# One token tile in the first block, global queries after it, and values' two parts in one matmul

## The chip, the cores and the metric

The kernel runs on one core of a Trainium2 chip. The metric is the device time of one execution in microseconds, from the first to the last instruction of that core with what lies around them; the median of several executions counts. The core's engines run side by side, each in its own order: TensorE (PE, with its weight loads as PEld), VectorE (DVE), ScalarE (ACT), GpSimd (POOL) and SyncE (SP), whose queue begins transfers. They wait for one another by semaphores.

## The reference

Windowed attention with global tokens is followed by a two-layer feed-forward over all 4352 tokens:

```python
k_all, v_all = concat([k_g, k_l]), concat([v_g, v_l])          # 8 batches, 8 heads, 32 global + 512 local, 64 wide
out_g = softmax(q_g @ k_all.T * scale) @ v_all                 # global queries see everything
s_ll  = where(|i - j| <= 32, q_l @ k_l.T * scale, -1e9)        # local queries see a window
out_l = softmax(concat([q_l @ k_g.T * scale, s_ll])) @ concat([v_g, v_l])
x = concat([out_g, out_l]) as (4352, 512)
h = x @ w_in                                                   # 512 -> 2048, weights drawn as float64
y = (h * sigmoid(h)) @ w_out                                   # 2048 -> 512
```

## The kernel before

The tokens are 34 tiles of the feed-forward (32 of 128 local tokens, two that gather the 128 global tokens of four batches each). The feed-forward takes them in blocks (`SIZES`): block 0 has two tiles, then ten of three, the last of two. A block runs 16 iterations f over the hidden width: `first_layer` makes h for 128 hidden units from four chunks, `second_layer` of the iteration before adds to one bank for each tile. Block 0 works in plain float32, whose matmuls the trace shows as two records each. Later blocks work on float32 split into a high and a low part (`w_hi`, `w_lo`, `xh`, `xl`), with three products per chunk in a faster format.

Attention is 128 steps k, a step being two heads (u = 0, 1) of one pair of the eight, for one tile of 128 queries; four steps make a tile and 16 a batch. A step loads `raw` (queries and keys) and `vraw`, makes scores s (`st_scores`, L345), a softmax with two exponentials (L353), turns the probabilities on TensorE (`st_turn`, t, L378 or L380) into `pt`, and multiplies with the values (`st_out`, o, L423). The 32 columns beside each 128 belong to the global queries' own share of that chunk, and are summed into `acc`. Steps before KF = 24 are whole: one float32 product. From 24 on values and probabilities are split, three products each (`vhi`, `vlo` against `pt_hi`, and `vhi` against `pt_lo`), 12 matmuls a step. Scores are split from 24 on too, in an earlier form up to ND = 28. Split steps carry `probs` through a transfer (`rr`), whole ones don't. For each batch the global queries' scores (`g_scores`, gs), softmax (`g_soft`) and turning (`g_turn`, gt and gu, into `pgt`) stand ahead of that batch's local steps; batches before GF = 2 are whole.

Weights come as float64 words, 32 halves of 512 KB. `load_weights` loads a half on SP's queue, ScalarE takes its upper words (L179), VectorE puts the bits together (L181, L182). `split_weights` then makes `w_hi` on ScalarE (L192) and `w_lo` on GpSimd (L193), after each iteration of block 0.

What sets the order: each piece of attention gets a due time, the pieces are sorted, and `fill` sets them between the feed-forward's matmuls, so that a block's iterations carry the steps of the next block. TensorE's order is that of the program; the other engines' instructions are ordered by a scheduler, except those that are held in program order. Ahead of block 0's matmuls stand the steps of its own tiles. PSUM banks for attention are one each for scores, turned tiles and values (with more of them before block 0 starts).

Of the kernel before, what the change touches and what calls it, by code (L numbers as in the profile page):

```python
# [20 lines left out]
P = 128  # L21
# [3 lines left out]
W = 224  # L25
# [27 lines left out]
MOVE0, TURN0 = (0.1, 0.8), (1.5, 3.6)  # L53
START = dict(head=0.55, gap=0.0, late=-0.65, first=1.8)
# [4 lines left out]
def attention_moe_kernel(ctx: ExitStack, tc: tile.TileContext, qk0_in, qk_in, v_in, gqk, wts, out):  # L59
# [102 lines left out]
    w_32, w_hi, w_lo, w_next = [], [], [], [0, 0]  # L162

    def load_weights():
        f, c0 = w_next
        if c0 == 0:
            w_32.append(const.tile([P, 2 * DM], F32, tag=f"ws{f + 1}", name=f"w{f}") if f + 1 < NF else xtiles(0)[1])
        w_next[:] = (f, DM) if c0 == 0 else (f + 1, 0)
        w = w_32[f][:, c0 : c0 + DM]
        raw = scratch(SCRATCH + (2 * f + c0 // DM) % (NF - SCRATCH), I32, f"raw_w{f}_{c0}")  # L170
        load = nc.sync.dma_start(out=raw, in_=wts[f, :, c0 : c0 + DM].bitcast(I32))
        if 2 * f + c0 // DM < NF - SCRATCH:
            tc.keep_in_program_order(load)

        words = raw.rearrange("p (n w) -> p n w", w=2)
        nc.scalar.activation(w, words[:, :, 1].bitcast(F32), AF.Prelu, scale=2.0**-112, alpha=-(2.0**32))  # L179
        wi, low = w.bitcast(U32), words[:, :, 0].bitcast(U32)  # L180
        nc.vector.tensor_scalar(out=low, in0=low, scalar1=29, scalar2=None, op0=ALU.logical_shift_right)  # L181
        nc.vector.scalar_tensor_tensor(out=wi, in0=wi, scalar=3, in1=low, op0=ALU.logical_shift_left,  # L182
                                       op1=ALU.bitwise_or)

    def split_weights(f):
        taken.add(f)
        w_hi.append(const.tile([P, 2 * DM], F32R, tag=f"wh{f}", name=f"w_hi{f}"))
        w_lo.append(const.tile([P, 2 * DM], F32R, tag=f"ws{f}", name=f"w_lo{f}"))
        for c0 in range(0, 2 * DM, DM):
            sl = slice(c0, c0 + DM)  # L190
            hi, lo, w = w_hi[f][:, sl], w_lo[f][:, sl], w_32[f][:, sl]
            nc.scalar.copy(out=hi, in_=w)  # L192
            nc.gpsimd.tensor_tensor(out=lo, in0=w, in1=hi.bitcast(F32), op=ALU.subtract)  # L193
# [20 lines left out]
    def g_scores(b, p):  # L214
        did(("scores", b, p), *([("turn" if b <= GF else "move", b - 1, p // 2)] if b else []))
# [36 lines left out]
    def g_move(b, hh):  # L252
# [4 lines left out]
        r1 = two.tile([P, SG], F32R, tag="rg", name=f"rg1_{b}_{hh}")  # L257
        nc.sync.dma_start(out=r0.bitcast(F32), in_=pgs[hh][:, : 4 * P])
        nc.sync.dma_start(out=r1.bitcast(F32), in_=pgs[hh][:, 4 * P :])
        state["rg", hh] = r0, r1  # L260

    def g_turn(b, hh):
        whole = b < GF
        if whole:
            r0, r1, idt = pgs[hh], pgs[hh][:, 4 * P :], ident.bitcast(F32)
        else:
            (r0, r1), idt = state.pop(("rg", hh)), ident
        did(("turn", b, hh), ("turn", b, 0) if hh else ("last", b - 1))
# [8 lines left out]
        nc.scalar.copy(out=pgt[:, 0:4, hs, :], in_=tb.rearrange("p (t h q) -> p t h q", t=4, h=4))  # L277
        tb = attbank("s", f"gu{b}_{hh}")
        nc.tensor.transpose(tb[:SG, :P] if whole else tb[:SG, :P].bitcast(F32R), r1, idt)
        nc.scalar.copy(out=pgt[:SG, 4, hs, :], in_=tb[:SG, :P].rearrange("p (h q) -> p h q", h=4))  # L280
# [4 lines left out]
    def st_load(k, b, c, pr):  # L285
        raw = raw_tile(f"raw{k}", k < KF)
# [6 lines left out]
    def st_vload(k, b, c, pr):  # L293
        if k < KF and k % 2:
            vraw = two.tile([P, 2, 2, D], F32, tag="vhi" if k % 4 == 1 else "vlo", name=f"vraw{k}")
# [5 lines left out]
    def st_split(k, b, c, pr):  # L301
        if k < KF:
            return
# [3 lines left out]
        if k < ND:  # L307
            n = QW + W
            nc.scalar.copy(out=qk[:, :n], in_=raw[:, :n])
            (nc.gpsimd if k < ND else nc.vector).tensor_tensor(out=klo[:, :n], in0=raw[:, :n], in1=qk[:, :n].bitcast(F32), op=ALU.subtract)  # L310
            return
        nc.scalar.copy(out=qk, in_=raw)  # L312
        (nc.gpsimd if k < ND else nc.vector).tensor_tensor(out=klo[:, :KW], in0=raw[:, QW:], in1=qk[:, QW:].bitcast(F32), op=ALU.subtract)
        nc.vector.tensor_tensor(out=qk[D:, :QW], in0=raw[D:, :QW], in1=qk[D:, :QW].bitcast(F32), op=ALU.subtract)

    def st_vsplit(k, b, c, pr):
# [3 lines left out]
        vhi = two.tile([P, 2, 2, D], F32R, tag="vhi", name=f"vhi{k}")  # L320
        vlo = two.tile([P, 2, 2, D], F32R, tag="vlo", name=f"vlo{k}")
# [3 lines left out]
        tiles["v", k] = vhi, vlo  # L325

    def st_scores(k, b, c, pr):
        if k < KF:
# [4 lines left out]
        for u in range(2):  # L333
            o = s[:, u * W : (u + 1) * W]
            qs = slice(u * P, (u + 1) * P)
            if k < KF:
                terms = [(raw[:, qs], raw[:, QW : QW + W])]
            elif k < ND:
                ks = slice(QW, QW + W)
                terms = [(qk[:, qs], qk[:, ks]), (qk[:, qs], klo[:, ks]), (klo[:, qs], qk[:, ks])]  # L340
# [27 lines left out]
    def st_turn(k, b, c, pr):  # L368
# [12 lines left out]
        t4 = t.rearrange("p (u a q) -> p u a q", u=2, a=2)  # L381
        if whole:
            pt = tiles["pt", k] = pt_whole(k)
            if c == NC - 1:
                nc.gpsimd.memset(pt[:, :, 1, P:], 0.0)
            nc.scalar.copy(out=pt[:, :, :, :P], in_=t4)
        else:
            pt_hi, pt_lo = pt_tiles(k)
            nc.scalar.copy(out=pt_hi[:, :, :, :P], in_=t4)
# [299 lines left out]
```

## Time and profile before

| | us |
|---|---|
| median of 3 runs (1088.55 to 1090.19) | 1089.91 |
| the profiled run | 1086.34 |
| its span, first to last instruction | 1084.6 |
| TensorE busy | 1053.5 (97%) |
| VectorE / ScalarE / GpSimd busy | 727.4 / 693.0 / 146.5 |

Matmuls overlap in the trace: the duration of one is not its price, and the price is read from the start of the next. A busy TensorE does not mean one at its peak. The chain of work that ended last is 93% TensorE over the span. Profiles show one execution; the sum in the prediction is made against its span.

### The profile page before, as it was taken

The page shows a single profiled execution, that of the slowest core. Times are in us where ns is not written, and L with a number is a line of the kernel's source. Part 1 is how long each engine was busy: PE and PEld are TensorE (multiplying, and loading weights), DVE is VectorE, ACT ScalarE, POOL GpSimd, SP SyncE. Part 2 cuts the span into 40 slices and gives each one's busy share as a digit, 9 for nine tenths or more (in the row PEclk, how much of TensorE's full clock was granted, in tenths as well). Part 3 has the DMA queues.
Part 4 walks back from the last instruction along what each step waited for, and adds up shares of the span by engine and source line. Part 5 has one row for each costly group of instructions (what it writes and reads, how often), then busy time and mean ns, then how long its engine had stood idle before and what let it go on. Part 6 is the DMA issues. An engine that isn't in the chain of part 4 may idle for free.

```text
span 1084.6 us, 20466 instructions
## 1 busy us (share of the span) xinstructions
PE 1053.5 (97%) x6568; PEld 934.9 (86%) x6568; DVE 727.4 (67%) x2367; ACT 693.0 (64%) x1845; POOL 146.5 (14%) x360
## 2 busy tenths in 40 slices
PE   6878999999999999999999999999999999999998
PEld 4645778989999999999999999998999999999997
DVE  5974355777677777666777877786778867753322
ACT  7875456767677766656766766776677776653232
POOL 3123542111100110000110100001000111000000
PEclk8989999999999999999999999999999999999999
DMA  9961112343334333332433433443344433310000
GB/s 351 380 189 59 57 59 76 119 146 125 111 112 142 124 107 115 116 115 82 140 110 122 149 111 109 138 135 108 111 141 125 141 114 112 112 60 20 1 30 20
DMA packets 69611, 127.29 MB, mean 117 GB/s; under 512 B 9344, under 2 KB 29312, under 8 KB 69504
## 3 DMA queue, kind: packets, MB, share of 16 engines
q1 hardware_dynamic: 69504, 125.99, 36.1%
q8 instruction: 52, 0.85, 0.3%
q14 instruction: 55, 0.45, 0.1%
HBM read 86.44 MB, written 8.91 MB: 88 GB/s over the span
## 4 chain that ended last, share of the span: by engine, by line
PE 93%; ACT 3%; DVE 2%; issue 1%; DMA 1%; ACTq 0%; DVEq 0%
PE h L563 33%; PE out L588 12%; PE out L590 11%; PE out L589 11%; PE o L423 10%; PE s L345 6%; PE t L380 3%; PE h L557 2%; PE out L586 2%; PE t L378 1%; DMA raw_w<-in_wts_dram 1%; PE gs L226 1%; PE gs L228 1%; ACT w_hi L192 1%; ACT w L179 1%
## 5 line engine op out<-in xcount | busy, mean ns | idle before, releaser
L563 PE MATMUL h<-xh,w_hi 128*128 128x384 f32 (+1 forms) x704 | 236.8, 336 | 0.0
L563 PE MATMUL h<-xh,w_lo 128*128 128x384 f32 (+1 forms) x704 | 233.5, 332 | 0.0
L563 PE MATMUL h<-xl,w_hi 128*128 128x384 f32 (+1 forms) x704 | 233.1, 331 | 0.0
L569 ACT ACTIVATE t<-h 128x384 f32<-128x384 f32 (+1 forms) x192 | 90.7, 472 | 207.3 <-PE h L563 189.4
L588 PE MATMUL out<-w_hi,gh 128*128 128x512 f32 x512 | 210.6, 411 | 0.0
L590 PE MATMUL out<-w_hi,gl 128*128 128x512 f32 x512 | 201.3, 393 | 0.0
L589 PE MATMUL out<-w_lo,gh 128*128 128x512 f32 x512 | 200.3, 391 | 0.0
L571 DVE SCALAR_TENSOR_TENSOR t<-t,h 128x384 f32<-128x384 f32 (+1 forms) x176 | 95.2, 541 | 132.6 <-ACT t L569 131.9
L563 PEld LDWEIGHTS h<-xl,w_hi 128*128 128x128 f32 x704 | 132.6, 188 | 5.4 <-issue 0.5
L563 PEld LDWEIGHTS h<-xh,w_hi 128*128 128x128 f32 x704 | 132.5, 188 | 5.4 <-issue 0.7
L400 POOL CAST pt_hi<-pgt 128x64 fp32r<-128x64 f32 (+1 forms) x132 | 39.1, 308 | 724.4 <-PE o L423 706.1
L563 PEld LDWEIGHTS h<-xh,w_lo 128*128 128x128 f32 x704 | 132.3, 188 | 0.0
L576 DVE TENSOR_TENSOR gl<-t,gh 128x384 fp32r<-128x384 f32 (+1 forms) x176 | 96.8, 550 | 46.6 <-PE out L590 42.5
L349 DVE CUSTOM_DVE_ANT_0 probs<-s,mask 128x224 f32<-128x224 f32 x244 | 85.0, 384 | 62.0 <-PE s L345 61.4
L353 ACT ACTIVATE probs<-probs,st 128x224 f32<-128x224 f32 x244 | 115.7, 475 | 11.2 <-DVE st L349 10.5
L590 PEld LDWEIGHTS out<-w_hi,gl 128*128 128x128 f32 x512 | 96.1, 188 | 22.3 <-DVE gl L576 0.3
L589 PEld LDWEIGHTS out<-w_lo,gh 128*128 128x128 f32 x512 | 97.0, 189 | 10.5
L588 PEld LDWEIGHTS out<-w_hi,gh 128*128 128x128 f32 x512 | 96.4, 188 | 10.6 <-ACT gh L575 0.4
L575 ACT CAST gh<-t 128x384 fp32r<-128x384 f32 (+1 forms) x176 | 88.3, 501 | 21.8 <-DVE t L571 17.3
L434 ACT CAST xh<-o 64x128 fp32r<-64x128 f32 x240 | 61.3, 256 | 42.5 <-PE o L423 29.4
L312 ACT CAST qk<-raw 128x704 fp32r<-128x704 f32 x100 | 78.2, 782 | 15.9 <-PE s L345 15.6
L435 DVE TENSOR_TENSOR xl<-o,xh 64x128 fp32r<-64x128 f32 x240 | 67.3, 280 | 30.9 <-ACT xh L434 27.4
(117 smaller groups left out, 1937.3 us busy)
## 6 DMA issues: line engine op xcount, KB each, us to landing
raw<-in_qk_dram SPq DMA_DIRECT2D x100, 352.0 KB, 3.0
rr<-probs SPq DMA_DIRECT2D x104, 256.0 KB, 2.3
raw_w<-in_wts_dram SPq DMA_DIRECT2D x32, 512.0 KB, 6.3
vraw<-in_v_dram SPq DMA_DIRECT2D x128, 128.0 KB, 2.4
raw_g<-in_gqk_dram SPq DMA_DIRECT2D x32, 304.0 KB, 2.9
out_dram<-o SPq DMA_DIRECT2D x32, 256.0 KB, 2.3
raw<-in_qk_dram SPq DMA_DIRECT2D x28, 240.0 KB, 4.8
rg<-pg SPq DMA_DIRECT2D x12, 256.0 KB, 2.4
```

Source lines behind the costliest of these rows:

```text
L312: nc.scalar.copy(out=qk, in_=raw)
L349: nc.vector.tensor_tensor_reduce(out=p[:, u, :W], in0=s[:, u * W : (u + 1) * W], in1=mask_of[c], scale=-SCALE, scalar=3.0e38, op0=ALU.add, ...
L353: nc.scalar.activation(p[:, u, :W], p[:, u, :W], AF.Exp, bias=st[:, u : u + 1], scale=-1.0, accum_out=st[:, 2 + u : 3 + u])
L423: nc.tensor.matmul(o[:D, u * wide : u * wide + m], v[:, a, u, :], pt[:, u, a, :m], start=(i == 0), stop=(i == len(terms) - 1))
L563: nc.tensor.matmul(h[:, :nt], wt, x[:, c, :nt], start=(i == 0), stop=(i == 3 * NCC - 1))
L569: nc.scalar.activation(t[:, :nt], h[:, :nt], AF.Tanh, scale=0.5)
L571: nc.vector.scalar_tensor_tensor(out=out[:, :nt], in0=t[:, :nt], scalar=1.0, in1=h[:, :nt], op0=ALU.add, op1=ALU.mult)
L575: nc.scalar.copy(out=gh[:, :nt], in_=t[:, :nt])
L576: nc.vector.tensor_tensor(out=gl[:, :nt], in0=t[:, :nt], in1=gh[:, :nt].bitcast(F32), op=ALU.subtract)
L588: nc.tensor.matmul(o, gh[:, sl], wh, start=(f == 0), stop=False)
L589: nc.tensor.matmul(o, gh[:, sl], wl, start=False, stop=False)
L590: nc.tensor.matmul(o, gl[:, sl], wh, start=False, stop=(f == NF - 1))
```

## The change

Block 0 takes one tile and the others three each. In `KF` 24 becomes 16 (steps 16 to 23 are split for values and probabilities), in `GF` 2 becomes 3, and scores stay whole up to step 27. The global queries of batch 0 come after block 0's own four steps, which leave their 32 columns out; `g_late` adds that share with eight small products. The values' high and low parts lie side by side in one tile `vv`, which one matmul takes as 128 stationary columns; the output's upper 64 rows hold the low part's product, and are added to the lower 64 through a tile `xs`. The last 32 keys of the global queries' probabilities are kept split in `pgh`, `pgl`, and no longer moved by a transfer of their own. Weight loads are begun by ScalarE on its own queue (`fetch_weights`) and joined later (`join_weights`), all held in program order; the weights' split begins at iteration 11 and goes on into block 1, one f an iteration.

```diff
-SIZES = (2, 3, 3, 3, 3, 3, 3, 3, 3, 3, 3, 2)
+SIZES = (1,) + (3,) * 11
-KF = 24
-GF = 2
+KF = 16
+GF = 3
-LOOK = 5
-FIRSTW, PACE, WAT = 2, 1.0, -1.5
+FETCH, LOOK = 4, 2
+SPLIT0, SPLITS = 11, 1.0
...
-        load = nc.sync.dma_start(out=raw, in_=wts[f, :, c0 : c0 + DM].bitcast(I32))
+        load = nc.scalar.dma_start(out=w_raw[i], in_=wts[i // 2, :, sl].bitcast(I32))
+        hold(load)
...
+        hold(nc.scalar.activation(w, words[:, :, 1].bitcast(F32), AF.Prelu, scale=2.0**-112, alpha=-(2.0**32)))
...
+            hold(nc.scalar.copy(out=hi, in_=w))
+            hold(nc.gpsimd.tensor_tensor(out=lo, in0=w, in1=hi.bitcast(F32), op=ALU.subtract))
...
-        nc.sync.dma_start(out=r1.bitcast(F32), in_=pgs[hh][:, 4 * P :])
...
+        nc.tensor.transpose(tb[:SG, :P], pgs[hh][:, 4 * P :], ident.bitcast(F32))
+        for i in range(2):
+            rows, src = slice(SG * (2 * hh + i), SG * (2 * hh + i + 1)), tb[:SG, QG * i : QG * (i + 1)]
+            nc.scalar.copy(out=pgh[rows, :], in_=src)
+            nc.vector.tensor_tensor(out=pgl[rows, :], in0=src, in1=pgh[rows, :].bitcast(F32), op=ALU.subtract)
...
     def st_split(k, b, c, pr):
-        if k < KF:
+        if k < ND:
             return
...
-        vhi = two.tile([P, 2, 2, D], F32R, tag="vhi", name=f"vhi{k}")
-        vlo = two.tile([P, 2, 2, D], F32R, tag="vlo", name=f"vlo{k}")
+        vv = two.tile([P, 2, 2, 2, D], F32R, tag="vv", name=f"vv{k}")
+        vhi, vlo = vv[:, :, :, 0, :], vv[:, :, :, 1, :]
...
-                terms = [(v, pt_hi, a) for a in range(2) for v in (vhi, vlo)] + [(vhi, pt_lo, a) for a in range(2)]
+                nc.tensor.matmul(o[:, at], vv[:, a, u].rearrange("p t d -> p (t d)"), pt_hi[:, u, a, :m],
+                                 start=(a == 0), stop=(a == 1))
+                nc.tensor.matmul(o[:D, at], vv[:, a, u, 0], pt_lo[:, u, a, :m], start=False, stop=(a == 1),
+                                 skip_group_check=(a == 1))
...
+        xs = work.tile([P, wide], F32, tag="xs", name=f"xs{k}")
         for u in range(2):
+            at = slice(u * wide, (u + 1) * wide)
             rows = slice(D * u, D * (u + 1))
+            nc.scalar.copy(out=xs[rows, :], in_=o[D:, at])
+            nc.vector.tensor_tensor(out=xs[rows, :], in0=o[:D, at], in1=xs[rows, :], op=ALU.add)
+        nc.scalar.copy(out=xh[:, pr, sl], in_=xs[:, :P])
+        nc.vector.tensor_tensor(out=xl[:, pr, sl], in0=xs[:, :P], in1=xh[:, pr, sl].bitcast(F32), op=ALU.subtract)
+        if c == 0:
+            nc.gpsimd.tensor_copy(out=gdst, in_=xs[:, P:])
+        else:
+            nc.gpsimd.tensor_tensor(out=gdst, in0=xs[:, P:], in1=gdst, op=ALU.add)
...
+                while w_next[1] < 2 * min(NF, f + LOOK):
+                    join_weights()
+                while w_next[0] < 2 * min(NF, f + FETCH):
+                    fetch_weights()
...
+            while len(w_hi) < NF and SPLIT0 + SPLITS * len(w_hi) <= NF * n + f:
+                split_weights(len(w_hi))
             g = first_layer(n, f)
...
-        if n == 0:
-            split_weights(f)
```

On TensorE the values of step 24 (o24) stood like this before, for the first head and the start of the second:

```order
L423 MATMUL o24_1838<-pt_hi_1795,vhi24_1732 64x160
L423 MATMUL o24_1838<-pt_hi_1795,vlo24_1733 64x160
L423 MATMUL o24_1838<-pt_hi_1795,vhi24_1732 64x128
L423 MATMUL o24_1838<-pt_hi_1795,vlo24_1733 64x128
L423 MATMUL o24_1838<-pt_lo_1797,vhi24_1732 64x160
L423 MATMUL o24_1838<-pt_lo_1797,vhi24_1732 64x128
```

The last figures are output rows by moving columns. Now the same head takes four matmuls, two of them with 128 output rows:

```order
L448 MATMUL o24_2066<-pt_hi_1237,vv24_1957 128x160
L450 MATMUL o24_2066<-pt_lo_1239,vv24_1957 64x160
L448 MATMUL o24_2066<-pt_hi_1237,vv24_1957 128x128
L450 MATMUL o24_2066<-pt_lo_1239,vv24_1957 64x128
```

On ScalarE, in the middle of block 0, joins (L179) and splits (L192) of weights stood where the scheduler put them, before, among exponentials and copies:

```order
L192 CAST w_hi7_1051<-w7_703 128x512
L179 ACTIVATE w11_950<-raw_w11_0_951 128x512
L434 CAST xh_1_601<-o10_738 64x128
L247 ACTIVATE pg0_123,gst1_0_731<-pg0_123,gst1_0_731 128x544
L192 CAST w_hi11_1300<-w11_950 128x512
L434 CAST xh_1_601<-o10_738 64x128
L179 ACTIVATE w11_950<-raw_w11_512_956 128x512
```

Now an iteration's two joins (L193) and two loads (L172) stand together there, with the loads two iterations ahead of their joins, and the splits come later:

```order
L193 ACTIVATE w6_536<-raw_w12_427 128x512
L193 ACTIVATE w6_536<-raw_w13_429 128x512
L172 DMA raw_w16_543<-in_wts_dram 128x1024
L172 DMA raw_w17_545<-in_wts_dram 128x1024
L369 ACTIVATE probs1_115<-probs1_115,st6_503 128x224
L459 CAST xh_1_513<-o4_515 64x128
L618 ACTIVATE t0_5_552<-h0_5_547 128x128
```

So the loads moved from SP's queue into ScalarE's order, between the joins and the tanh (L618) of block 0.

## Rows read from the trace of the kernel before

**Rows 1.** Stretches (us): length, busy us (count) by engine, TensorE clock, DMA share, GB/s

```profile
0.00:154.86 154.86, 130.43 (x572) 91.99 (x573) 97.17 (x329) 103.31 (x277) 51.25 (x82) 0.92 0.54 187
10.00:81.00 71.00, 54.47 (x247) 40.01 (x248) 59.81 (x199) 61.36 (x159) 13.13 (x22) 0.86 0.87 310
154.86:1084.60 929.74, 923.07 (x5998) 842.88 (x5996) 630.26 (x2039) 589.64 (x1569) 95.23 (x278) 1.00 0.34 106
...
10.00:45.00 35.00, 25.69 (x137) 21.08 (x138) 31.28 (x120) 32.04 (x90) 5.49 (x11) 0.85 1.03 388
```

**Rows 2.** Timeline of PE, 520 to 532 us: start, duration, engine, line, operation, tiles

```profile
521.88 0.24 PE L423 MATMUL o<-pt_hi,vhi 128*64 128x160 f32 x1
...
522.69 0.40 PE L563 MATMUL h<-xh,w_hi 128*128 128x384 f32 x1
...
523.28 0.34 PE L563 MATMUL h<-xh,w_hi 128*128 128x384 f32 x1
...
524.67 0.34 PE L563 MATMUL h<-xh,w_lo 128*128 128x384 f32 x1
...
531.38 0.46 PE L380 MATMUL t<-ident,rr 128*128 128x128 f32 x4
531.67 0.47 PE L588 MATMUL out<-w_hi,gh 128*128 128x512 f32 x1
```

**Rows 3.** Timeline of PE, 503 to 506 us, a step of the last chunk

```profile
503.03 0.26 PE L345 MATMUL s<-qk 128*128 128x224 f32 x1
...
503.46 0.41 PE L588 MATMUL out<-w_hi,gh 128*128 128x512 f32 x1
...
504.85 0.23 PE L423 MATMUL o<-pt_hi,vhi 128*64 128x160 f32 x1
...
505.74 0.43 PE L588 MATMUL out<-w_hi,gh 128*128 128x512 f32 x1
```

**Rows 4.** Timeline of PE in the last block, 1072 us, first layer

```profile
1072.57 0.28 PE L563 MATMUL h<-xl,w_hi 128*128 128x256 f32 x1
1072.69 0.28 PE L563 MATMUL h<-xh,w_lo 128*128 128x256 f32 x1
```

**Rows 5.** Timeline of PE where block 1 begins, 149 to 155 us

```profile
149.30 0.92 PE L345 MATMUL s<-raw 128*128 128x224 f32 x4
150.06 1.89 PE L557 MATMUL h<-x,w 128*128 128x256 f32 x8
151.88 1.19 PE L423 MATMUL o<-pt,vraw 128*64 128x160 f32 x8
153.00 1.12 PE L586 MATMUL out<-w,gh 128*128 128x512 f32 x2
153.96 0.60 PE L378 MATMUL t<-ident,probs 128*128 128x128 f32 x4
154.40 1.02 PE L586 MATMUL out<-w,gh 128*128 128x512 f32 x2
154.86 0.74 PE L563 MATMUL h<-xh,w_hi 128*128 128x384 f32 x1
```

**Rows 6.** Groups by line: operation, tiles, shapes, count, busy us, mean ns, idle before

```profile
L434 ACT CAST xh<-o 64x128 fp32r<-64x128 f32 x240 | 61.3, 256 | 42.5 <-PE o L423 29.4 <-DVE acc L442 4.1 <-DVE acc L440 4.0
```

**Rows 7.** Timeline of ACT, 18 to 21 us

```profile
18.73 0.66 ACT L179 ACTIVATE w<-raw_w 128x512 f32<-128x512 f32 x1
19.30 0.60 ACT L192 CAST w_hi<-w 128x512 fp32r<-128x512 f32 x1
19.81 0.48 ACT L353 ACTIVATE probs__116<-probs__116,st 128x224 f32<-128x224 f32 x1
...
20.29 0.47 ACT L353 ACTIVATE probs__116<-probs__116,st 128x224 f32<-128x224 f32 x1
```

**Rows 8.** Timeline of SP's queue, 21 us

```profile
20.92 0.38 SPq L171 DMA_DIRECT2D raw_w<-in_wts_dram  x1
```

**Rows 9.** DMA issues on the page: tiles, queue, operation, count, KB, us to landing

```profile
raw_w<-in_wts_dram SPq DMA_DIRECT2D x32, 512.0 KB, 6.3
```

More of the change, by code (lines that the diff above doesn't have):

```diff
@@ L381, in st_turn @@
         t4 = t.rearrange("p (u a q) -> p u a q", u=2, a=2)
+        if k < NPR:
+            pt = tiles["pt", k] = pt_whole(k)
+            nc.scalar.copy(out=pt[:, :, :, :P], in_=t4)
+            return
+        did(("last", b) if (c, pr) == (NC - 1, NPR - 1) else k, ("turn", b, pr // 2))
+        pgt, pgh, pgl = state["pgt"]
+        g = pgt[:, c, 2 * pr : 2 * pr + 2, :]
         if whole:
             pt = tiles["pt", k] = pt_whole(k)
+            nc.scalar.copy(out=pt[:, :, :, :P], in_=t4)
+            nc.gpsimd.tensor_copy(out=pt[:, :, 0, P:], in_=g)
@@ L384, in st_turn @@
             if c == NC - 1:
+                rows = slice(SG * pr, SG * (pr + 1))
+                hi, lo = (part.bitcast(F32)[rows, :].rearrange("p (u q) -> p u q", u=2) for part in (pgh, pgl))
                 nc.gpsimd.memset(pt[:, :, 1, P:], 0.0)
[L386 to L389, printed above, removed]
-            nc.vector.tensor_tensor(out=pt_lo[:, :, :, :P], in0=t4, in1=pt_hi[:, :, :, :P].bitcast(F32),
-                                    op=ALU.subtract)
@@ L425, in st_out @@
-        g0 = SG * (b % 4)
+            for a in range(2):
+                m = wide if (a == 0 or c == NC - 1) and k >= NPR else P
+                at = slice(u * wide, u * wide + m)
+                if whole:
+                    nc.tensor.matmul(o[:D, at], vraw[:, a, u, :], pt_f[:, u, a, :m], start=(a == 0), stop=(a == 1))
+                    continue
+                nc.tensor.matmul(o[:, at], vv[:, a, u].rearrange("p t d -> p (t d)"), pt_hi[:, u, a, :m],
+                                 start=(a == 0), stop=(a == 1))
+                nc.tensor.matmul(o[:D, at], vv[:, a, u, 0], pt_lo[:, u, a, :m], start=False, stop=(a == 1),
+                                 skip_group_check=(a == 1))
@@ new lines, in st_out @@
+        if whole:
+            for u in range(2):
+                rows = slice(D * u, D * (u + 1))
+                src, gsrc = o[:D, u * wide : u * wide + P], o[:D, u * wide + P : (u + 1) * wide]
+                if n == 0 and u:
+                    nc.vector.tensor_copy(out=xh[rows, pr, sl], in_=src)
+                else:
+                    nc.scalar.copy(out=xh[rows, pr, sl], in_=src)
+                if n:
+                    nc.vector.tensor_tensor(out=xl[rows, pr, sl], in0=src, in1=xh[rows, pr, sl].bitcast(F32),
+                                            op=ALU.subtract)
+                if k >= NPR:
+                    nc.vector.tensor_tensor(out=gdst[rows, :], in0=gsrc, in1=gdst[rows, :], op=ALU.add)
+            return
@@ L475, in put @@
         stream.append((when, fn, a))
-    for h in range(NPR):
-        due = START["head"] * h + (START["late"] if h > 1 else 0.0)
-        put(due - 0.6, g_load, 0, h)
-        put(due, g_split, 0, h)
-        put(due + START["gap"], g_scores, 0, h)
-        if h % 2:
-            put(due + START["gap"] + 0.2, g_soft, 0, h // 2)
-    at = START["first"]
     AHEAD = NPR * SIZES[0]
```

185 lines of the change are left out of this document (94 added, 91 removed).

## Prediction

> **What bounds the kernel now.** I read the stretches first, then TensorE's timeline at the seam between the first and the second block, then single matmuls, then ScalarE. The run has two parts. From 154.86 us on, where block 1 begins, TensorE is busy 923.07 of 929.74 us at full clock, and VectorE and ScalarE 630 and 590 us [rows 1]: here the end moves by what TensorE is given, and work on the other engines is hidden as long as it stays in time. Before that point TensorE is busy 130 of 155 us at a mean clock of 0.92, so part of it at the lower of its two levels (1.2 against 2.4 GHz). From 10 to 45 us three others are full at once: DMA 1.03 (388 GB/s), ScalarE 32.04 and VectorE 31.28 of 35 us [rows 1]. So I split the span into T, the start of block 1, and R, everything after it: 154.86 + 929.7 before. A matmul's own duration (230 to 400 ns) is latency; its price is the distance to the next start.
>
> **Prices on TensorE.** In steady work: 12 value matmuls with 160 and 128 moving columns take 0.81 us (521.88 to 522.69), in the last chunk, all 160 wide, 0.89 (504.85 to 505.74). Four turns take 0.29 (531.38 to 531.67). Four score matmuls take 0.43 (503.03 to 503.46), six of the second layer 1.39, so 0.232 each (503.46 to 504.85), eight of the first layer with 384 columns 1.39, so 0.174 each (523.28 to 524.67) [rows 2, 3]. With 256 columns one takes 0.12 [rows 4]. In float32, a record per pass: scores of a step 0.76 (149.30 to 150.06), its values 1.12 (151.88 to 153.00), its turns 0.44 (153.96 to 154.40), the second layer about 0.45 a record (153.00 to 153.96 for two) [rows 5].
>
> **The change in R, part by part.**
> (a) Block 0 has one tile instead of two. Before, by the order of instructions, scores up to step 21 and values up to step 19 stand ahead of block 1; now scores up to 17, values up to 15. Four steps move behind the seam: scores 4 x 0.76, turns 4 x 0.29, values 4 x 0.59 (priced below): 6.6 us more.
> (b) The second tile of block 0 (float32) becomes the third tile of the last block (split): 16 x 12 first-layer matmuls grow from 0.12 to 0.174 (10.4 us) and 16 x 3 second-layer matmuls come on top, at 0.232 (11.2): 21.6 us more. Block 0's last second layer, also behind the seam, loses two records: 0.9 less.
> (c) Steps 20 to 23 are split instead of whole: values 1.12 to 0.59, turns 0.44 to 0.29: 4 x 0.68 = 2.7 us less.
> (d) Values side by side, for the 104 steps from 24 on. Of 12 matmuls 8 stay; of these four have a 128-column stationary operand. No row shows one with 160 moving columns. With 128 columns on both sides the turns take 0.073 each; 32 columns more, at (0.174 - 0.12)/128 us a column, make 0.087. A narrow pair (160 and 128) is a sixth of 0.81, 0.135. A step costs 2 x (0.087 + 0.073) + 2 x 0.135 = 0.59, in the last chunk 4 x 0.087 + 4 x 0.074 = 0.65. Saved: 78 x 0.22 + 26 x 0.24 = 23.4 us. If the wide ones cost no more than narrow ones, a third of all goes: 78 x 0.27 + 26 x 0.30 = 28.9. I take 23.4, since the turns show a width of 128 to cost something.
> (e) Small: batch 2's global scores go back to one float32 product (some 0.3 us for each of four), its turns and the last 32 rows' turns become float32, and the scores of steps 24 to 27 go from six split matmuls (0.65) to one whole product (0.76): 2.4 us more together. The late global product for the first four steps is 8 small matmuls, within T.
> (f) What leaves TensorE loads others. A split step has three ScalarE copies and three VectorE operations where it had two and four, with the xs tile between them; GpSimd takes the sum for the global queries. At 256 ns a copy [rows 6] this is 0.3 us of ScalarE a step, about 3.5 us for a block's 12; ScalarE's share in R goes from 63% to some 68%. Also 22 of the 32 weight splits move behind the seam. The 12 small rg loads leave SP's queue and 8 rr loads of steps 16 to 23 join it; the DMA share there is 0.34, which hides them. TensorE covers all this unless it must wait for one of these operations; I put 4 us for such waits, with 0 and 12 as ends: 12 us is 1.3% of R, twice the 6.7 us that TensorE is not busy in R now.
> Sum: 6.6 + 21.6 - 0.9 - 2.7 - 23.4 + 2.4 + 4 = 7.6, so R = 929.7 + 7.6 = 937.3.
>
> **The change in T.** TensorE has to do, ahead of the seam, only about 74 us at the prices above (18 score steps 13.7, 16 turned 7.0, values 16, global 9.5, block 0 first layer 128 records of 0.11 = 14, second layer 32 of 0.45 = 14). It cannot have them so early: all 32 weight chunks (16.8 of some 26 MB, from the sizes of the loads: 32 of 512 KB, 18 of 240, 16 of 128, 8 of 304) must still be loaded and joined first. At the 388 GB/s of the full stretch 26 MB take 67 us. ScalarE was busy 103.3 us up to the seam [rows 1]. It loses 22 split casts (0.50 each, 19.30 to 19.81), 8 exponentials (0.48 with their read, 19.81 to 20.29) [rows 7], four steps' scaling, turned copies and value copies and half of each tanh (some 6), and gains small copies (1): 84 us. Now it also begins the 32 weight loads. What this costs on ScalarE no row shows; on SP's queue one takes 0.33 to 0.38 us [rows 8]. Bounds: 0 and 32 x 0.38 = 12 us, so 84 to 96. VectorE's 97 us lose some 7 (four softmaxes, four pairs of copies): 90. Nothing starts before about 7 us (an estimate: the first load, then the masks that GpSimd makes). At the 92% of ScalarE from 10 to 45 us this gives 7 + 90/0.92 = 105 to 7 + 96/0.92 = 111; if neither engine ever paused, 97 to 103. I take T = 104, between the two pairs, since the list of the slower engine is shorter by a fifth than before and its gaps were waits for others; ends 95 (just under a full VectorE) and 119 (7 + 96/0.86, ScalarE's 61.36 of 71 us from 10 to 81 [rows 1]). A queue of its own frees the weights from SP's order, where they stood between loads that wait for buffers, but it brings no more bytes while DMA is full. The waits added: a load in ScalarE's order waits for an earlier transfer, and joins, exponentials and tanh stand behind it. The landing takes 6.3 us [rows 9]; a load is begun two iterations (some 10 us) ahead of its join, which hides it.
> Span: 104 + 937.3 = 1041.3. The profiled run before is 1.7 us longer than its span, the median 3.6 above that run: 1041.3 + 1.7 + 3.6 = 1046.6.
>
> **The rivals.**
> 1. The wide weight loads are not hidden. If the interval of a load doubles with its columns, from the 0.06 of a narrow 128-column matmul to 0.12, a split step costs 4 x 0.12 + 0.27 = 0.75 and (d) brings 7.5 instead of 23.4: 1062. Against it: the turns load 128 columns each and follow at 0.073 [rows 2].
> The Trainium skill states this rule: in "TensorE: Matmul & The Clock Gate", LDWEIGHTS (loading the stationary operand), a weight load takes its number of columns over 1.2 ns, so 107 ns for 128 columns; an estimate by it makes the step 0.70 and the time some 10 us longer than forecast. The 0.073 us of the turns disagrees with it here.
> 2. ScalarE stalls on its own loads: if each of block 0's 16 iterations pays a landing (6.3) and two joins (0.57 each, 18.73 to 19.30 [rows 7]), 7.4 us, behind some 20 us for the first four steps (14 us of ScalarE work after the first 7, an estimate), T is 139: 1081. For it: one queue in order, with waits on transfers. Against it: two iterations of lead.
> 3. Better: the issue costs nothing and TensorE's shorter list lets ScalarE run full, T = 92; with (d) at 28.9 and no new waits, 1046 - 12 - 5.5 - 4 = 1025.
> 4. Slower: the value bank. Its output is now drained by four operations in turn (ScalarE, VectorE, ScalarE, VectorE) on a single bank that global scores and turns share. If TensorE waits w for it in each of the 112 split steps, the gain is gone at (1090 - 1046)/112 = 0.39 us a step; at 0.5 us the time is 1102. For it: both engines run in order, some 70% busy, so each of the four can queue. Against it: behind the seam steps are some 8 us apart (937/112), and four operations of 0.26 us [rows 6] are little over 1 us.
>
> **How the numbers follow.** Forecast 66% (1046), rival 1 8%, rival 2 9%, rival 3 10%, rival 4 5%, left over 2%. The range 1027 to 1070 holds the forecast with T from 95 to 119 and waits up to 12 us, rival 1, and most of rival 3; it leaves out rivals 2 and 4. A measurement here can tell 0.2% (2 us) from no change. All but rival 4 and the rest are faster: faster 0.93, same 0.02, slower 0.05.
>
> **What would show it.** First matmul of block 1 near 104 us; TensorE over 98% busy from there; the value matmuls of a split step at 0.59 us from first start to the next instruction (0.70 to 0.75: rival 1; 0.54: the better end); ScalarE over 85% busy from 10 us to the seam, with weight loads at some 0.3 us each or none. ScalarE idle behind weight transfers means rival 2, value matmuls waiting for xs rival 4. I am wrong if T is above 119, or if TensorE's idle time in R grows by more than 12 us.

## The result, and the profile after

The changed kernel takes 1093.20 us (median of 20 runs, 1088.43 to 1097.96), beside 1088.78 for the kernel before (20 runs, 1086.59 to 1090.19). The ratio is 1.0042, 95% interval 1.0028 to 1.0056: slower by 0.4%, where 1046 was forecast. Its runs spread over 9.5 us (those of the kernel before over 3.6), the longer ones at a lower mean granted clock (0.981 at 1097.56 us), and the profile is of one of the shortest (1088.63 us at 0.991, span 1086.8), which is the run that what follows explains.

The two stretches of the changed kernel, cut at the first split matmul of block 1 (columns as in [rows 1]):

```profile
0.00:126.07 126.07, 89.21 (x495) 65.44 (x495) 83.31 (x288) 81.76 (x229) 28.35 (x60) 0.96 0.66 223
126.07:1086.80 960.73, 944.44 (x5676) 860.90 (x5674) 666.12 (x1997) 653.14 (x1748) 161.23 (x420) 1.00 0.33 105
```

T fell by 28.8 us, to 126.07, and R grew by 31.0, to 960.73. Forecast were 104 and 937.3, so each missed by 22 to 23 us. Ahead of the seam no engine is full: VectorE and ScalarE are busy 83 and 82 of 126 us, and the DMA share is 0.66.

The waits of TensorE in the last iterations of block 0, 91 to 127 us (engine, what it would run, released by: us in all, times, longest):

```profile
PE o L444 <- DVE acc L464: 7.9, 1, 7.9
PE gt L291 <- DVE acc L464: 4.7, 2, 2.4
```

And the timeline of all engines in that stretch. The value bank (o) is drained for each head by a copy xh on ScalarE (L459) and by xl and acc on VectorE (L461, L464); L193, L195 and L196 are joins, L206 and L207 splits:

```profile
89.31 0.69 DVE L196 SCALAR_TENSOR_TENSOR w<-w,raw_w 128x512 uint32<-128x512 uint32 x1
89.70 2.83 POOL L207 TENSOR_TENSOR w_lo<-w,w_hi 128x512 fp32r<-128x512 f32 x2 [2.06 <-ACT w_hi L206]
89.91 1.50 DVE L195 TENSOR_SCALAR raw_w<-raw_w 128x512 uint32<-128x512 uint32 x1
91.53 1.56 DVE L196 SCALAR_TENSOR_TENSOR w<-w,raw_w 128x512 uint32<-128x512 uint32 x1
...
100.14 1.23 ACT L193 ACTIVATE w<-raw_w 128x512 f32<-128x512 f32 x2
...
101.27 1.12 ACT L206 CAST w_hi<-w 128x512 fp32r<-128x512 f32 x2
...
102.02 3.19 POOL L207 TENSOR_TENSOR w_lo<-w,w_hi 128x512 fp32r<-128x512 f32 x2 [4.18 <-ACT w_hi L206]
102.42 0.26 ACT L459 CAST xh<-o 64x128 fp32r<-64x128 f32 x1
102.52 1.57 DVE L196 SCALAR_TENSOR_TENSOR w<-w,raw_w 128x512 uint32<-128x512 uint32 x1
...
104.10 0.28 DVE L461 TENSOR_TENSOR xl<-o,xh 64x128 fp32r<-64x128 f32 x1
104.31 0.17 DVE L464 TENSOR_TENSOR acc<-o,acc 64x32 f32<-64x32 f32 x1
...
104.75 2.36 PE L444 MATMUL o<-pt,vraw 128*64 128x160 f32 x8 [7.90 <-DVE acc L464]
...
111.81 1.30 PE L444 MATMUL o<-pt,vraw 128*64 128x160 f32 x8
```

The second head's copy xh stands behind two joins and two casts on ScalarE, then xl and acc behind a join on VectorE. TensorE's next values need that bank, and scores and the first layer stand behind them. TensorE has nothing to run from 96.85 us on. When it goes on, it is at the lower of its two levels, 1.2 GHz: the granted clock is 0.50 from 102.0 to 108.8 us, and the eight value records take 2.36 us instead of the 1.30 at 111.81.

Behind the seam, a split step's values as TensorE's timeline shows them (answers to [rows 2]):

```profile
139.50 0.24 PE L448 MATMUL o<-pt_hi,vv 128*128 128x160 f32 x1
139.57 0.24 PE L450 MATMUL o<-pt_lo,vv 128*64 128x160 f32 x1
139.65 0.26 PE L448 MATMUL o<-pt_hi,vv 128*128 128x128 f32 x1
139.74 0.23 PE L450 MATMUL o<-pt_lo,vv 128*64 128x128 f32 x1
139.81 0.29 PE L448 MATMUL o<-pt_hi,vv 128*128 128x160 f32 x1
139.93 0.24 PE L450 MATMUL o<-pt_lo,vv 128*64 128x160 f32 x1
140.00 0.26 PE L448 MATMUL o<-pt_hi,vv 128*128 128x128 f32 x1
140.10 0.23 PE L450 MATMUL o<-pt_lo,vv 128*64 128x128 f32 x1
140.16 0.45 PE L637 MATMUL out<-w_hi,gh 128*128 128x512 f32 x1
```

From the first start to the next instruction this is 0.66 us, where 0.59 was forecast. Over all 112 split steps the distances from each value matmul to the next start add up to 78.2 us, 0.70 a step; before, 85.9 us for 104 steps, 0.83.

### The profile page after: what moved, and what is told of

The parts are those of the page before. It is cut to its first block, busy times and chain, and to the rows that moved or that the text cites. A ratio compares the mean times of both kernels' runs of the same rounds, so it can differ in the third digit from the quotient of the medians.

```text
span 1086.8 us, 19886 instructions
## 1 busy us (share of the span) xinstructions
PE 1033.7 (95%) x6168; PEld 926.3 (85%) x6168; DVE 749.4 (69%) x2285; ACT 734.9 (68%) x1977; POOL 189.6 (17%) x480
## 4 chain that ended last, share of the span: by engine, by line
PE 87%; DVE 4%; ACT 4%; issue 2%; DMA 1%; POOL 0%; ACTq 0%; DVEq 0%; POOLq 0%
PE h L612 33%; PE out L637 12%; PE out L639 11%; PE out L638 11%; PE s L357 5%; PE o L448 4%; PE o L450 3%; PE t L392 3%; DVE w L196 1%; PE o L444 1%; PE gs L240 1%; ACT probs L365 1%; DMA raw<-in_qk_dram 1%; ACT w_hi L206 1%; PE gt L291 1%
## 5 line engine op out<-in xcount | busy, mean ns | idle before, releaser
L612 PE MATMUL h<-xh,w_hi 128*128 128x384 f32 x704 | 241.4, 343 | 0.0
L612 PE MATMUL h<-xl,w_hi 128*128 128x384 f32 x704 | 238.3, 339 | 0.0
L612 PE MATMUL h<-xh,w_lo 128*128 128x384 f32 x704 | 238.3, 339 | 0.0
L637 PE MATMUL out<-w_hi,gh 128*128 128x512 f32 x528 | 219.6, 416 | 0.0
L618 ACT ACTIVATE t<-h 128x384 f32<-128x384 f32 (+1 forms) x192 | 90.6, 472 | 158.9 <-PE h L612 152.1
L620 DVE SCALAR_TENSOR_TENSOR t<-t,h 128x384 f32<-128x384 f32 x176 | 97.2, 552 | 113.1 <-ACT t L618 111.8
L625 DVE TENSOR_TENSOR gl<-t,gh 128x384 fp32r<-128x384 f32 x176 | 99.2, 563 | 46.1 <-PE out L639 40.4
L416 POOL CAST pt_hi<-pgt 128x64 fp32r<-128x64 f32 x112 | 37.7, 336 | 490.1 <-PE o L450 347.7
L624 ACT CAST gh<-t 128x384 fp32r<-128x384 f32 x176 | 89.8, 510 | 21.5 <-DVE t L620 18.8
L471 DVE TENSOR_TENSOR xs<-o,xs 64x160 f32<-64x160 f32 x224 | 70.7, 315 | 28.5 <-ACT xs L470 24.3
L327 ACT CAST qk<-raw 128x704 fp32r<-128x704 f32 x100 | 78.1, 781 | 16.3 <-PE s L357 14.9
L448 PE MATMUL o<-pt_hi,vv 128*128 128x160 f32 x448 | 87.7, 264 | 0.6 <-DVE xs L471 0.3
```

Source lines behind the costliest of these rows:

```text
L448: nc.tensor.matmul(o[:, at], vv[:, a, u].rearrange("p t d -> p (t d)"), pt_hi[:, u, a, :m], start=(a == 0), stop=(a == 1))
L612: nc.tensor.matmul(h[:, :nt], wt, x[:, c, :nt], start=(i == 0), stop=(i == 3 * NCC - 1))
L618: nc.scalar.activation(t[:, :nt], h[:, :nt], AF.Tanh, scale=0.5)
L620: nc.vector.scalar_tensor_tensor(out=out[:, :nt], in0=t[:, :nt], scalar=1.0, in1=h[:, :nt], op0=ALU.add, op1=ALU.mult)
L624: nc.scalar.copy(out=gh[:, :nt], in_=t[:, :nt])
L625: nc.vector.tensor_tensor(out=gl[:, :nt], in0=t[:, :nt], in1=gh[:, :nt].bitcast(F32), op=ALU.subtract)
```

## The experiments

T and R are those of each profiled run, and depend on the clock granted in it; the time is the median, the ratio is to the kernel before, run beside it.

| kernel | time, us | ratio (95%) | T | R |
|---|---|---|---|---|
| before | 1088.78 | | 154.9 | 929.7 |
| after | 1093.20 | 1.0042 (1.0028 to 1.0056) | 126.1 | 960.7 |
| before, values side by side | 1077.94 | 0.9909 (0.9896 to 0.9921) | 151.1 | 923.6 |
| the same, all operands wide | 1091.20 | 1.0030 (1.0018 to 1.0041) | 150.0 | 938.6 |
| the same, grouped | 1077.15 | 0.9897 (0.9884 to 0.9910) | 151.8 | 922.0 |
| after, later splits | 1090.06 | 1.0015 (0.9999 to 1.0031) | 119.2 | 965.0 |
| after, later splits, earlier loads | 1090.35 | 1.0034 (1.0015 to 1.0052) | 124.0 | 960.6 |
| after, narrow values | 1099.19 | 1.0092 (1.0077 to 1.0107) | 132.7 | 970.0 |
| after, no fixed places | 1113.71 | 1.0230 (1.0211 to 1.0249) | 148.8 | 961.9 |
| after, loads on SP | 1097.07 | 1.0081 (1.0068 to 1.0095) | 135.1 | 960.9 |
| after, three value banks | 1079.65 | 0.9926 (0.9901 to 0.9951) | 114.4 | 958.9 |
| the same, later splits | 1079.26 | 0.9915 (0.9895 to 0.9935) | 110.9 | 963.4 |
| the same, earlier joins | 1080.26 | 0.9927 (0.9914 to 0.9940) | 114.2 | 962.5 |
| before, side by side, second bank | 1067.22 | 0.9814 (0.9800 to 0.9828) | 140.7 | 923.0 |

### What a wide value matmul costs

Values side by side alone, in the kernel before:

```
+ nc.tensor.matmul(o[:, at], vv[:, a, u].rearrange("p t d -> p (t d)"), pt_hi[:, u, a, :m], ...)
+ nc.tensor.matmul(o[:D, at], vv[:, a, u, 0], pt_lo[:, u, a, :m], ...)
+ xs (ACT copy, DVE add), xh, xl from xs; acc on GpSimd
+ last 32 rows' turns kept as pgh, pgl, no transfer of their own
```

> The kernel before with one part of the change alone: values' hi and lo parts side by side (eight matmuls a split step instead of twelve, the xs tile, the sum for the global queries on GpSimd, the last 32 rows' turns without a transfer). Blocks, whole steps, load queues and joins stay as before. 104 split steps. Theory A (term (d) was mis-sized: the trace after shows 0.108 us for a wide matmul with 160 moving columns, 0.096 with 128, so 0.68 to 0.70 a step instead of 0.81): 104 x 0.12 = 12.5 us off TensorE, less 2 to 6 us of new waits, so 1076 to 1082 us, ratio 0.988 to 0.994. Theory B (the prediction's 0.59 holds here, and the change after lost it to other work): 23 us less waits, 1066 to 1072, ratio 0.979 to 0.985. Theory C (rival 4: the chain of four operations on the value bank gives it back): 1087 or more, ratio 0.998 or above, with TensorE waiting for VectorE's xs sum or for pt_lo in many steps.

It took 1077.94 us: theory A. The values' distances are 71.6 us for 104 steps, 0.69 a step, 14.3 less than before. R fell by only 6.1, since the distances behind first- and second-layer matmuls grew by 8.8 us. Of these, 4.2 us are time in which TensorE is not busy, ahead of values, scores and global turns; the rest is spread over the layers' own matmuls and was not explained. T fell by 3.8, at a mean clock of 0.97 ahead of the seam instead of 0.92; no split value step stands there.

With the second matmul wide as well:

```
- nc.tensor.matmul(o[:D, at], vv[:, a, u, 0], pt_lo...)
+ nc.tensor.matmul(o[:, at], vv[:, a, u].rearrange("p t d -> p (t d)"), pt_lo...)
```

> As the run with the values side by side alone, but the matmul with pt_lo uses the 128-column operand too (it also adds vlo times pt_lo, which the others leave out), so every stationary operand of a step has 128 columns. It tells apart why a wide matmul took 0.108 and 0.096 us in the changed kernel when turns with 128 columns follow at 0.073. Theory A1 (what costs is the change between operands of 128 and of 64 columns): at 0.087 and 0.073 a step takes 4 x 0.160 = 0.64 us, 0.04 to 0.06 less than with narrow ones between, so some 5 us faster than that run. Theory A2 (a wide load costs this much each time): 4 x (0.108 + 0.096) = 0.82 us a step, as much as before, so some 14 us slower than that run, about 1090 us with the waits.

1091.20 us, 13 us more than with narrow ones: theory A2. A step in this kernel (TensorE's timeline):

```profile
528.41 0.24 PE L431 MATMUL o<-pt_hi,vv 128*128 128x160 f32 x1
528.48 0.28 PE L433 MATMUL o<-pt_lo,vv 128*128 128x160 f32 x1
528.59 0.26 PE L431 MATMUL o<-pt_hi,vv 128*128 128x128 f32 x1
528.69 0.27 PE L433 MATMUL o<-pt_lo,vv 128*128 128x128 f32 x1
528.80 0.29 PE L431 MATMUL o<-pt_hi,vv 128*128 128x160 f32 x1
528.93 0.27 PE L433 MATMUL o<-pt_lo,vv 128*128 128x160 f32 x1
```

In these lines the next one follows after 0.07 to 0.13 us. Over the whole run the mean distance behind the pt_lo matmuls is 0.1115 us, with 160 moving columns as with 128; narrow, in the run above, it is 0.075 and 0.063. Behind the pt_hi ones it is 0.106 and 0.097, beside 0.105 and 0.096 there. No change of width is left here, so it is the 128-column stationary operand that costs. That its load does, and not its 128 output rows, is argued only: the second price does not grow with the moving columns.

The wide ones first, then the narrow ones:

```
 for u, a: matmul(o[:, at], vv wide, pt_hi)
+for u, a: matmul(o[:D, at], vv narrow, pt_lo)
```

> As the run with the values side by side alone, but with another order in a split step: the four wide matmuls of both heads first, then the four narrow ones with pt_lo; two changes of width a step instead of eight. Theory A1 (the change of width costs): 0.32 for the wide and 0.27 for the narrow ones and two changes at some 0.03, 0.62 to 0.65 us a step, 3 to 7 us faster than that run. Theory A2 (each wide load costs 0.108 or 0.096 wherever it stands): 0.41 + 0.27 = 0.68 us, the same time as that run within 2 us; the narrow ones at 0.075 and 0.063 would still be the same.

In this order the second head's group is opened while the first head's is still being added to, and the results lack part of the sums (that the order is the reason is not shown). The run stands for its time alone; number and shapes of the matmuls are the same. 1077.15 us, within 1 us of the run with both kinds in turn, and the value distances differ by 0.8 us in all: A2 again.

The trace before already tells two kinds of 128-column load apart. Its groups of PEld (line, operation, tiles, shape, count, busy, mean ns), then in the changed kernel:

```profile
L423 PEld LDWEIGHTS o<-pt_hi,vhi 128*64 128x64 f32 x416 | 56.0, 135 | 2.8 <-issue 0.5
L380 PEld LDWEIGHTS t<-ident,rr 128*128 128x128 f32 x416 | 46.7, 141 | 7.5
L563 PEld LDWEIGHTS h<-xl,w_hi 128*128 128x128 f32 x704 | 132.6, 188 | 5.4 <-issue 0.5
```

```profile
L448 PEld LDWEIGHTS o<-pt_hi,vv 128*128 128x128 f32 x448 | 82.6, 189 | 4.6 <-issue 1.1 <-POOL vv L338 0.7
L450 PEld LDWEIGHTS o<-pt_lo,vv 128*64 128x64 f32 x448 | 61.4, 137 | 4.9 <-issue 2.2
```

A turn's load has 128 columns too but takes 141 ns, little more than a 64-column one; an ordinary 128-column load takes 188. The turns, from which the wide price was taken, are another kind of load.

The values taken apart again in the changed kernel:

```
- wide vv matmul, xs, acc on GpSimd
+ vv[:, a, u, v] for v in 0, 1 (64 columns each); copies straight from o
```

> The changed kernel with its values taken apart again: twelve matmuls with 64-column operands a split step, no xs tile, the copies and the sum for the global queries as in the kernel before. All else stays changed. Theory A (a wide value step saves 0.137 us, as the run with the values alone shows in its sum of distances, 14.3 us for 104 steps, and some 40% of that goes in waits): 112 x 0.137 = 15 us more TensorE work and 4 to 8 us fewer waits, so 1093 + 7 to 11 = 1100 to 1104. Theory C (in this kernel the xs chain costs as much as it saves): 1095 or less. Theory B (the prediction's 0.22 a step): 1093 + 25 = 1118 less a few us of waits, 1112 or more.

1099.19 us, just under theory A's 1100; by the two ratios 0.5% (5.4 us) over the changed kernel. R is 9.2 us longer and the values' distances 14.5 us. So the saving holds here too, less some 5 us that go elsewhere. Ahead of the seam the clock of its profiled run is 0.88, where the changed kernel has 0.96, so its T is not compared.

### What makes T

Splits three iterations later:

```
-SPLIT0, SPLITS = 11, 1.0
+SPLIT0, SPLITS = 14, 1.0
```

> The changed kernel with one number changed: the splits of the weights into two parts begin three iterations later in block 0 (14 instead of 11), so GpSimd's subtractions and ScalarE's casts for them move behind the seam. Theory D (T missed its forecast because from 86.7 us on these splits stand in ScalarE's order ahead of value copies, and because VectorE's join operations beside GpSimd's take 1.5 us instead of 0.69): the gap of 7.9 us at 104.75 shrinks or goes, iterations 14 and 15 come back to 6 to 7 us, T falls from 126 to 110 to 116, and the time to some 1080; R gets a few us of it back if block 1's second layer waits for a split. Rival E (T is set by something else, such as loads or TensorE at half clock): T stays at 122 or more and the time within 3 us of 1093.

T fell by 6.8, to 119.2, but R grew by 4.2: 1090.06 us, between the ranges of D and E. In the changed kernel 6 of the 64 VectorE join operations (L195, L196) take 1.26 to 1.57 us, all of them beside a w_lo subtraction of GpSimd; here it is 1. The Trainium skill, "SBUF — State Buffer", Who interferes with whom, says that a VectorE instruction with two SBUF inputs contends with a GpSimd instruction that reads SBUF; the join at 102.52 (1.57 us beside w_lo, against 0.69 at 70.19 without one) agrees. Two of the six are shifts (L195) with one tensor input, which that sentence does not cover. The changed kernel without a subtraction beside the join, and then the run with later splits behind the seam (columns as in [rows 1]):

```profile
70.19 0.69 DVE L196 SCALAR_TENSOR_TENSOR w<-w,raw_w 128x512 uint32<-128x512 uint32 x1 [0.22 <-ACT w L193]
```

```profile
372.20:375.40 3.20, 3.20 (x13) 3.20 (x12) 0.41 (x2) 0.69 (x2) 0.00 (x0) 0.50 0.00 0
635.00:638.20 3.20, 3.20 (x12) 3.20 (x11) 0.43 (x2) 0.60 (x3) 0.00 (x0) 0.50 0.03 7
```

Little of R's growth comes from the splits that moved there: block 1 takes 98.2 us instead of 97.4. Another 3.1 us lie in blocks 3 and 6, in these two stretches at 1.2 GHz. Each begins 0.8 to 1.3 us after the start of a global turn ahead of which TensorE had stood still for 1.96 us. The changed kernel has the same two standstills and a clock of 1.00 after them, and the next run, with splits as late as here, has R at 960.6. So it is not shown that the splits take back behind the seam what they free in T.

Loads one iteration earlier on top:

```
-FETCH, LOOK = 4, 2
+FETCH, LOOK = 5, 2
```

> The changed kernel with splits three iterations later (as in the run on splits alone, T 119, time 1090) and with each weight load begun one iteration earlier (5 ahead instead of 4). In that run's chain the largest piece of the last iterations is a weight transfer of 7.1 us from 92.67 us on. Theory L (T's end waits for that load, which stands late in ScalarE's order): T falls to 111 to 115, the time to 1082 to 1087. Rival (the last iterations are set by VectorE's and ScalarE's chain through joins and softmax, the load only seems last): T stays at 118 or more, the time at 1088 or more.

T 124.0, time 1090.35: theory L falls. The last load begins at 88.4 us instead of 92.7, and the end came no earlier (at a clock of 0.94 ahead of the seam, against 0.97). The load that stood last in the chain of the run before was not what held it.

No fixed places for joins, splits and loads:

```
-hold = tc.keep_in_program_order
+def hold(instruction): return instruction
```

> The changed kernel without its fixed places: joins, splits and weight loads are put into each engine's order by the scheduler's own priorities instead of staying where the program has them. Theory H (value copies and exponentials stand behind joins and splits that are held ahead of them, and this makes T): T falls to 105 to 118, the time to 1075 to 1088. Rival J (the chain through TensorE itself sets block 0's pace: in the trace after, its chain from 48 to 88 us is mostly TensorE's own work, some 5.4 us an iteration): T stays within 4 us of 126 and the time between 1089 and 1097. It may also come out longer, if the scheduler puts joins later: 1098 or more.

T 148.8, time 1113.71: theory H falls, and the third branch came. TensorE now waits 14.2 us for pt copies of ScalarE (the longest 10.9) and 8.8 for acc. All places were freed at once here, so this does not tell which of them helps; the scheduler's own are worse together.

Weight loads in SP's queue:

```
-load = nc.scalar.dma_start(out=w_raw[i], ...)
+load = nc.sync.dma_start(out=w_raw[i], ...)
```

> The changed kernel with the weight loads begun by SP, in its queue, instead of ScalarE. This undoes the queue alone. Theory Q (the own queue brings T something, since in SP's order a weight load stands behind loads that wait for buffers): T 130 to 140, the time 1097 to 1107. Theory N (the queue makes no difference; T's length is made by the order of work on ScalarE, VectorE and TensorE): T within 4 us of 126, the time 1089 to 1097. Theory S (issuing costs ScalarE time, up to 32 x 0.38 = 12 us): T 114 to 122, the time below 1089.

T 135.1, R as in the changed kernel, time 1097.07: theory Q, in the time at the edge of its range. By the ratios the queue is worth some 4 us; at equal mean clock (0.990 and 0.991) it is some 8, which fits T. Most of T's 9 us lie at its start: the first layer begins at 31.38 us instead of 23.99. Busy time leaves out the issuing of loads, so what that costs ScalarE is read from the changed kernel's timeline of ScalarE and its queue:

```profile
61.78 0.33 ACTq L172 DMA_DIRECT2D raw_w<-in_wts_dram  x1
62.18 0.69 ACT L193 ACTIVATE w<-raw_w 128x512 f32<-128x512 f32 x1
62.23 0.37 ACTq L172 DMA_DIRECT2D raw_w<-in_wts_dram  x1
62.76 0.68 ACT L193 ACTIVATE w<-raw_w 128x512 f32<-128x512 f32 x1
```

The second issue runs beside the first join; no time of ScalarE's own is seen to go to it here.

Three banks instead of one for values and global turns while block 0 runs (it has one tile, so two output banks lie empty):

```
+elif spare and kind == "o":
+    i = next(banks[kind]) % 3
+    if i: return ps_out.tile([P, 512], F32, tag=f"out{i}", name=name)
```

> The changed kernel with two more banks for values, late values and global turns while block 0 runs: block 0 has one token tile, so the output banks of tiles 2 and 3 lie empty there, and these results rotate over three banks instead of one. The splits stay where the change put them. Theory V (TensorE stands still in the last iterations because the single value bank is drained late, by ScalarE's and VectorE's copies that stand behind joins and splits: 7.9, 2.3 and 2.4 us of waits for acc at the end of T, 14 us in all before the seam): T falls by 8 to 14, to 112 to 118, R unchanged, time 1079 to 1086. Rival W (the bank only passes on a delay that the joins make anyway, since the first layer needs the joined weights): the waits move to the first layer or to the values' own inputs, T stays at 123 or more, time 1089 or more.

1079.65 us: theory V. T fell by 11.7, to 114.4, and R by 1.9. TensorE's waits from 91 to 115 us in this run:

```profile
PE s L362 <- issue: 2.9, 1, 2.9
PE o L449 <- issue: 2.7, 1, 2.7
```

The 12.6 us of waits for acc are gone, 5.6 us of others have come.

With later splits on top:

```
-SPLIT0, SPLITS = 11, 1.0
+SPLIT0, SPLITS = 14, 1.0
```

> The run with three value banks in block 0, and with the splits three iterations later (14 instead of 11). Theory V: both causes of the late stretch are taken away together, T 104 to 112, R 961 to 966, time 1072 to 1080. Rival W: T as with the later splits alone, 119 or more, time 1087 or more. A third way: the splits that now stand in block 1 delay its second layer more than with one bank, since block 1 starts earlier; then T falls and R grows by as much.

T 110.9, R 963.4 and the time of 1079.26 are all within theory V's bounds. Beside the run with one change less, T is 3.5 us shorter and R 4.5 longer, no gain that can be measured. That looks like the third way, but block 1 took only 1.7 us more of R (96.8 instead of 95.1); 3.1 us lie in blocks 3 and 6 again, at a granted clock of 0.50 from 361.5 to 364.9 and from 624.3 to 627.7 us.

Joins and loads one iteration earlier on top of that:

```
-FETCH, LOOK = 4, 2
+FETCH, LOOK = 5, 3
```

> The run with three value banks and later splits in block 0, with joins three iterations ahead of their use instead of two, and loads five instead of four. In that run the last iterations before the seam still take 8.1 and 6.8 us, and TensorE waits 3.1 us for joined weights, in three gaps. Theory K (what is left of the last iterations is the joins' lateness): T falls from 110.9 to 105 to 108, time 1073 to 1077. Theory M (what is left is the chain of softmax, turns and global heads through ScalarE and VectorE, and earlier joins stand in its way): T 110 or more, time 1078 or more.

T 114.2, time 1080.26: in the bounds of theory M. The loss lies early: the fourth iteration begins at 46.8 us instead of 41.3. That the joins stand in the way of other work there is theory M's reason and was not tried apart.

A second bank in the kernel before with values side by side (block 0 has two tiles there, so one output bank is empty):

```
+elif spare and kind == "o" and next(banks[kind]) % 2:
+    return ps_out.tile([P, 512], F32, tag="out2", name=name)
```

> The run with the values alone side by side (two tiles in block 0, all else as before), with one more bank for values and global turns in block 0: the third tile's output bank lies empty there. It tells whether the single value bank already cost time ahead of the seam before the change, or costs only since the change made block 0 short. In that run's trace, from 40 us to the seam, TensorE waits 7.1 us in five gaps ahead of value matmuls and 1.8 us ahead of a global score, for reasons that the profile does not name or for acc. Theory V1 (these are the bank): T falls from 151 by 4 to 9, the time to 1069 to 1074. Theory V2 (ScalarE and VectorE are the limit there with two tiles, so the bank only passes their delay on): T within 3 us of 151, time 1076 to 1080.

1067.22 us, below both theories' bounds and 1.9% faster than the kernel before: the best version here. T fell by 10.4, to 140.7, R stayed. With two tiles in block 0, too, the single bank cost time ahead of the seam. TensorE is now nearly full there (40 to 140 us, columns as in [rows 1]):

```profile
40.00:140.00 100.00, 97.28 (x459) 69.18 (x460) 67.83 (x229) 71.03 (x192) 43.03 (x52) 1.00 0.44 142
```

## Why the prediction was wrong

**T: 104 forecast, 126.1 measured.** The lists of work were no longer than I said: ScalarE 81.8 us where I gave 84 without the issues, VectorE 83.3 where I gave 90. The step that failed is the rate: I let the slower engine run at the 92% of 35 chosen microseconds of [rows 1] over its whole list. By the same sum it ran at 70%: 7 + 83.3/0.70 = 126. The first line of [rows 1] has that rate already: ScalarE's 103.31 us are 70% of the 154.86 less 7. I took its gaps for waits that would go with a shorter list, and most of them stayed. (No run tells whether the two rates agree by more than chance.)

What makes the gaps is shown for a part. Each iteration's values and global turns pass from engine to engine through one bank, and each engine works in order; with three banks T is 11.7 us shorter, half of the 22. That one tile leaves less other work to fill the gaps is argued, not shown. Later splits take another 3.5 us off T. Some 7 us over the forecast remain even with both, and I can't say from what: half-clock stretches after a gap, and the last global heads, are seen there but were not tried apart.

**Rival 4 had the mechanism, in the wrong place.** I looked for the value bank's wait behind the seam, at every split step, and there no wait of a value matmul for xs is longer than 0.3 us. I did not ask the question ahead of the seam, where steps come every 5 to 6 us and a drain can stand behind joins of 0.57 to 1.57 us. Two global waits and one for values cost 12.6 us there. **Rival 2** does not hold: ScalarE waits 1.1 us for weight transfers ahead of the seam, where it had to wait 6.3 for each.

The global heads share that bank, and behind the seam they do wait for it. The profile names xs for 3.5 us of TensorE's waits there. Two more waits of 1.96 us, ahead of global turns, carry no name:

```profile
374.20 0.40 PE L639 MATMUL out<-w_hi,gl 128*128 128x512 f32 x1
376.14 0.32 DVE L471 TENSOR_TENSOR xs<-o,xs 64x160 f32<-64x160 f32 x1
376.56 0.50 PE L291 MATMUL gt<-ident,rg 128*128 128x128 f32 x4 [1.96 <-issue]
```

Their operands rg had landed at 355.67 and 616.42 us. The turn starts 0.10 us after VectorE's last reading of the value bank, and so does the other one (638.25); in the kernel before, the one such wait (753.96) ends 0.10 us after acc. So 7.4 of the 16.3 us in which TensorE is not busy in R are waits for the value bank.

**The own queue** was right in sign: it frees the weights from SP's order, for 9 us of T in the profiled runs and some 4 in the medians.

**R: 937.3 forecast, 960.7 measured.** About half of the 23.4 us missed is values side by side, the other half the moved work: I forecast 21.2 us for the values (the moved work alone sums to 28.8, as shown below, the whole with its waits to 7.6), and taking them apart again costs 9.2.

Term (d) was mis-sized: 0.137 us a step instead of 0.22, so 14.3 instead of 23.4 in the run that has it alone. Rival 1 was nearer with its mechanism, a wide load that shows. I argued against it with the turns' 0.073 us, which are another kind of load. The Trainium skill, "TensorE: Matmul & The Clock Gate", LDWEIGHTS (loading the stationary operand), gives columns over 1.2 ns, 107 ns for 128; the measured 0.1115 us agrees, and so does the estimate of 0.70 a step by it, which I had set aside.

Term (f), the new waits, was put at 4 us with 12 as its end. TensorE's time not busy in R grew from 6.7 to 16.3, by 9.6. That is inside the end, but not the value taken. With narrow values it is 12.9, so values side by side account for 3.4 of the 9.6 (4.2 in the run that has them alone), and the moved work for 6.2.

Terms (a) to (c) and (e), the moved work, were too low. With narrow values R is 40.2 us over before. For that kernel (a) is 7.5 with old values, (b) 21.6 less 0.9, (c) minus 1.8 and (e) 2.4: 28.8. Of the 11.4 missing, 6.2 are time in which TensorE is not busy (12.9 against 6.7 us); its waits for acc on the value bank, found as above, come to 6.4 us there and to 2.0 before. Another 4.7 us are an estimate from the granted clock: three stretches of 2.6, 3.4 and 3.4 us behind the seam have 0.50, which is half of their time lost, and the kernel before has none there but at its very end. My sum has the 4 us of (f) for all waits, and nothing for the clock.

**The sum.** Both parts missed the same way, 22 us in T and 23 in R, against a forecast gain of 43. The moved work costs 28.8 by my own terms, as much as T gave (28.8), and 40 measured. With narrow values the change would pay only if T came nearer 104; as measured, it pays with three value banks, and the values pay more without the moved work, as the last run shows.

## What to carry to other kernels

When work is shortened ahead of a point, don't divide what is left by the rate that an engine had in its fullest stretch: take the rate over the whole list, and ask which buffer hands it from engine to engine, and what stands ahead of its drain in each in-order queue. A spare bank can be worth more than the work removed. Take an operation's price from a row of the same kind, including its weight load's row, not from one that merely has the same shape.

## What the runs showed that I had not expected

- Behind a matmul with a 128-column stationary operand and 128 to 160 moving columns the next follows after 0.10 to 0.11 us, with a 64-column one after 0.06 to 0.075. For turns with 128 columns it is 0.073, with load records of 140 ns instead of 188.
- VectorE's join took 1.57 us at 102.52, instead of 0.69 at 70.19, beside a GpSimd subtraction; even the shift with one tensor input (L195) took 1.50 at 89.91, against 0.42 at 100.86.
- The issue of a load by ScalarE (0.37 us in its queue, at 62.23) runs beside ScalarE's own instruction.
- A standstill of TensorE of 1.96 us, at the same turn, was followed by a granted clock of 0.50 for 3.4 us in some profiled runs and of 1.00 in others; the first kind has 1.5 to 1.6 us more in that block.
